# Pooled attention and a gated product on one core: the first w3 tile in two halves, and 71 steps in other places of the written order

## The chip, the core and the metric

The kernel runs on one core of a Trainium2 chip. The metric is the device time in microseconds (us). TensorE (PE) does the matmuls and transposes, VectorE (DVE), ScalarE (ACT) and GpSimd (POOL) the elementwise work, and SyncE (SP) issues the transfers between memory and the core.

## What is computed

The reference, cut to its core (the weights come as float64):

```
k_p = k.reshape(8, 8, 72, 8, 64).mean(axis=3)      # 576 tokens pooled to 72 keys
v_p = v.reshape(8, 8, 72, 8, 64).mean(axis=3)
attn = softmax(q @ k_p^T / 8)                      # 8 batches, 8 heads
x = (attn @ v_p), heads side by side               # 4608 x 512
a = x @ w1;  b = x @ w2                            # w1, w2: 512 x 1024
out = ((a * b) @ w3) @ w_out                       # w3: 1024 x 1024, w_out: 1024 x 512
```

## The kernel before

**W phase.** The kernel first forms W = w3 @ w_out, so that each token needs only (a*b) @ W. A float64 tile is loaded as pairs of 32-bit words. ACT converts the high word (`high`, line L190), ACT or DVE takes the bits of the low word (`low`, L196 on ACT, L199 on DVE), and DVE joins them (`conv_b`, L203). w3 comes in 16 tiles (s = 0 to 15). PE turns each one by four transposes (`w_turn`, L253 or L255), ACT rounds the turned tile into its high part (`w3_hi`, L265), and the low part is the rest: for tiles in `LO3_PE` PE subtracts (`w3_sub`, one matmul at L258) and ACT copies (`w3_lo`, L273), for the others DVE subtracts (L261). The tiles of w_out take `ro_high`, `ro_low`, `ro_conv`, `ro_hi` (L239) and `ro_lo` (L243). Twelve matmuls per tile (`w_mm`, L1068) add three passes (high by high, high by low, low by high) for each of four column blocks. Transposes of the identity whose result nobody reads (`warm`, L281) occupy PE before the first product.

**Chunks.** The 4608 tokens are 12 chunks of 384. Chunks 0 to 3 are done plainly (`a_mm`, `b_mm` at L787, `b_post` at L807, `g_lo` at L817, `out_mm` at L835). The others go in pairs M = 2 to 5 with seven products per column block j (`prod(M, j, i)`, L976) in the manner of Strassen. Mixed weights for these (`mix_sum` L881, `mix` L887 to L889) are formed once on POOL or DVE and stored in `ws`. For each pair `load_u(M, j, g)` (L958) brings group g of block j into a ring: groups 0, 1 and 2 are 512 KB each and share five slots, group 3 is 256 KB with a slot of its own. Group 1 serves the products i = 2 and 4, group 0 those with i = 0 and 1. `out_some(m, j, ...)` (L851) adds to the output of a chunk, `out_post` stores it.

**Attention.** For chunk n `tr_q` (L390) turns q, `s_mm` (L543) makes scores, `soft1` to `soft4` the softmax, `prep_k`, `prep_v`, `prep_v3` (L499), `vr_sub` and `prep_vr2` (L530) prepare the pooled keys and values for the products at L739. `load_k`, `load_v` and `load_vr` bring them in.

**What sets the order.** The program is a list `plan` of steps. A tuple of numbers says in which order they are issued, and every engine works through its own instructions in that order. All loads and most stores pass through SP's queue. Eight completion semaphores go round among the transfers, so a transfer is issued only when the one eight places ahead has landed, and when its buffer is free.

```
    for i in SEQUENCE:
        fn, args = plan[i]
        fn(*args)
```

Of the kernel before, what the change touches and what calls it, by code (L numbers as in the profile page):

```python
# [8 lines left out]
F32 = mybir.dt.float32  # L9
# [10 lines left out]
def kernel(  # L20
# [46 lines left out]
    LO3_PE = [0, 2, 3, 4, 6, 7]  # L67
# [12 lines left out]
        "r3_low": {(0,), (1,), (2,), (4,), (13,), (15,)},  # L80
# [91 lines left out]
    def load_w3(s):  # L172
        h, j = divmod(s, NJ)
        raw["w3", s] = raw_cell(s % 4)
        nc.sync.dma_start(
            out=raw["w3", s].rearrange("p (i c) -> p i c", i=4),
            in_=w3r[h * 512:(h + 1) * 512, 2 * j * P:2 * (j + 1) * P].rearrange("(i p) c -> p i c", p=P))
# [27 lines left out]

    def w_tiles(s):
        if s == NJ + 4:
            t = early.tile([P, 24], F32, name="space")
            nc.gpsimd.memset(t, 0.0)
        if "wt" not in stage:  # L210
            stage["wt"] = [t[:, i] for t, x in (
                (p1.tile([P, x, 512], I32, tag=tag, name="wt"), x)
                for tag, x in (("PTh", 3), ("PTx", 4))) for i in range(x)]
        if s < NJ:
            stage["wo", s] = stage["wt"][s % 4], f(stage["wt"][4 + s % 3])
        stage["w3", s] = W_cell(0, 4 + s % 4, I32), W_cell(1, 4 + s % 4, F32)

    def r3_high(s):
        w_tiles(s)
        high(raw["w3", s], stage["w3", s][1])  # L220

    def r3_low(s):
        low(raw.pop(("w3", s)), stage["w3", s][0], other("r3_low", s))

    def r3_conv(s):
        conv_b(*stage["w3", s])
# [20 lines left out]
    def w_turn(s):  # L247
        r = f(stage.pop(("w3", s))[0])
        ps = tp[s] = patt.tile([P, 512], F32, tag="att", name="att")
        for it in range(4):  # L250
            o, i = ps[:, it * P:(it + 1) * P], r[:, it * P:(it + 1) * P]
            if s in LO3_PE:
                nc.tensor.matmul(out=o, lhsT=i, rhs=ident, is_transpose=True, start=it == 0, stop=it == 3)  # L253
            else:
                nc.tensor.transpose(out=o, in_=i, identity=ident)  # L255
# [7 lines left out]
    def w3_hi(s):  # L263
        w3t[s] = hl_cell(4 + s % 4)
        nc.scalar.copy(out=w3t[s][0], in_=tp[s])  # L265

    def w3_sub(s):
        if s in LO3_PE:
            less(tp[s], w3t[s][0])

    def w3_lo(s):
        if s in LO3_PE:
            nc.scalar.copy(out=w3t[s][1], in_=tp.pop(s))  # L273
        else:
            minus(w3t[s][1], tp.pop(s), w3t[s][0])
# [884 lines left out]
    for i in range(1, 7):  # L1160
        at("L", F0 - 5, warm, i, 5)
    for u in range(NJ + 2):
        k = F0 + 2 * (u - 2)
        if u < NJ:
            at("P", k, r3_high, u)
            at("P", k, r3_low, u)
            at("P", k, ro_high, u)
# [4 lines left out]
        if u < NJ:  # L1172
            at("P", k, r3_conv, u)
        if 1 <= u < NJ + 1:
            at("P", k, w_turn, u - 1)
            at("P", k, w3_hi, u - 1)
# [4 lines left out]
        if 1 <= u < NJ + 1:  # L1181
            at("P", k, w3_sub, u - 1)
            at("P", k, ro_hi, u - 1)
            at("P", k, w3_lo, u - 1)
    for s in range(NS):
        k = F0 + 2 * s
        if s < NJ:
            at("L", k - 11, load_w3, s)
# [144 lines left out]
    for b in range(1, B):  # L1333
# [189 lines left out]
```

## Time and profile before

| | us |
|---|---|
| median of 3 runs | 742.46 (741.91 to 743.19) |
| the profiled execution | 740.11 |
| its span | 738.3 |
| PE busy in the span | 720.7 |
| DVE, ACT, POOL busy | 523.8, 362.1, 189.1 |

The span is what the trace shows from the first to the last instruction; 1.8 us of the profiled execution lie outside it. PE is busy nearly all the time, so a gap of PE is what an order can remove.

### The profile page before, as it was taken

To read this page: it belongs to the slowest core of one execution; us is meant where nothing else is said; L and a number is where in the kernel's file an instruction comes from. 1 tells how busy PE (TensorE), PEld (TensorE's weight loads), DVE (VectorE), ACT (ScalarE), POOL (GpSimd) and SP (SyncE) were. 2 spreads that over 40 slices of the span, in tenths; PEclk is the share of its full clock that TensorE was granted. 3 is DMA by queue.
4 is the path that set the end of the run, shared out by engine and by line. 5 is a ranking of instruction groups with operands and counts; after the bars stand their busy time and mean duration, and the time that the engine had idled before them with its cause. 6 is when DMAs were issued, how large, how long until landed. Compare 5 with 4: busy or idle time off the path is not lost.

```text
span 738.3 us, 12016 instructions
## 1 busy us (share of the span) xinstructions
PE 720.7 (98%) x3992; PEld 665.9 (90%) x3992; DVE 523.8 (71%) x1042; ACT 362.1 (49%) x1140; POOL 189.1 (26%) x241
## 2 busy tenths in 40 slices
PE   7999999999999999998999999999999999999997
PEld 6788989899989999998999899899898999899996
DVE  3988898869767968887568877488887576643342
ACT  6888786534334544663355553355554254421221
POOL 2343865434506506203313011220030100000000
PEclk9999999999999999999999999999999999999999
DMA  9999590174457556798785739966358563166511
GB/s 320 348 285 288 154 255 30 59 205 118 108 141 249 155 152 194 198 293 224 221 263 151 186 106 277 252 204 175 86 194 276 139 208 115 34 228 233 173 35 69
DMA packets 138733, 136.59 MB, mean 185 GB/s; under 512 B 76080, under 2 KB 104240, under 8 KB 138672
## 3 DMA queue, kind: packets, MB, share of 16 engines
q1 hardware_dynamic: 138528, 135.69, 63.0%
q8 instruction: 32, 0.52, 0.3%
q14 instruction: 29, 0.24, 0.1%
q10 hardware_dynamic: 144, 0.13, 0.1%
HBM read 99.35 MB, written 24.12 MB: 167 GB/s over the span
## 4 chain that ended last, share of the span: by engine, by line
PE 78%; DVE 9%; DMA 4%; POOL 4%; ACT 3%; issue 2%; SPq 0%; DVEq 0%; POOLq 0%; ACTq 0%
PE a L976 17%; PE o L835 14%; PE att L976 8%; PE o L851 8%; PE a L787 6%; PE b L787 6%; PE b L976 5%; PE att L543 4%; PE att L739 4%; PE o L1068 3%; DMA ring<-ws 2%; DMA PTx<-T 1%; DVE mx L559 1%; POOL VR L530 1%; DMA raw<-in_moe_w_out_dram 1%
## 5 line engine op out<-in xcount | busy, mean ns | idle before, releaser
L976 PE MATMUL a<-X,ring 128*128 128x384 f32 x768 | 157.0, 340 | 1.4 <-DVE g L1009 0.7
L976 PEld LDWEIGHTS a<-X,ring 128*128 128x128 f32 x768 | 134.7, 189 | 7.0 <-DVE g L1009 1.7
L835 PE MATMUL o<-Wc,gh 128*128 128x512 f32 (+1 forms) x384 | 118.6, 390 | 0.0
L581 ACT ACTIVATE E<-att,mx 128x72 f32<-128x72 f32 (+1 forms) x264 | 80.7, 324 | 32.8 <-DVE mx L559 21.2
L482 POOL TENSOR_TENSOR st<-st 72x512 f32<-72x512 f32 (+2 forms) x32 | 42.7, 1335 | 162.0 <-DMA st<-in_v_dram 101.3
L835 PEld LDWEIGHTS o<-Wc,gh 128*128 128x128 f32 x384 | 70.2, 188 | 11.7 <-DVE ob L868 0.2
L976 PE MATMUL att<-X,ring 128*128 128x384 f32 x384 | 78.6, 341 | 2.0 <-DMA ring<-ws 2.0
L835 PE MATMUL o<-Wc,gl 128*128 128x512 f32 (+1 forms) x192 | 74.6, 389 | 1.2 <-DVE gl L817 1.1
L787 PE MATMUL b<-xT,hl 128*128 128x384 f32 x384 | 73.2, 340 | 0.1
L787 PE MATMUL a<-xT,hl 128*128 128x384 f32 x384 | 72.4, 337 | 0.0
L976 PEld LDWEIGHTS att<-X,ring 128*128 128x128 f32 x384 | 68.0, 190 | 3.5 <-DVE R L630 2.4
L787 PEld LDWEIGHTS a<-xT,hl 128*128 128x128 f32 x384 | 66.7, 188 | 0.5
L787 PEld LDWEIGHTS b<-xT,hl 128*128 128x128 f32 x384 | 66.2, 188 | 0.7 <-DVE a L807 0.4
L851 PE MATMUL o<-Wc,gh 128*128 128x512 f32 x192 | 61.6, 393 | 0.0
L817 DVE TENSOR_TENSOR gl<-a,gh 128x384 fp32r<-128x384 f32 x64 | 41.1, 646 | 22.7 <-ACT gh L812 18.2
L581 ACT ACTIVATION_READ_ACCUMULATOR E<-att,mx 128x1 f32 (+1 forms) x264 | 55.2, 209 | 0.0
L812 ACT CAST gh<-a 128x384 fp32r<-128x384 f32 x64 | 33.0, 517 | 43.8 <-DVE a L1004 14.9
L543 PE MATMUL att<-kbd,qT 128*128 128x144 f32 (+1 forms) x320 | 49.3, 286 | 0.6 <-DVE qT L390 0.6
L543 PEld LDWEIGHTS att<-kbd,qT 128*128 128x128 f32 (+1 forms) x320 | 45.3, 179 | 2.9 <-DVE qT L390 0.9
L835 PEld LDWEIGHTS o<-Wc,gl 128*128 128x128 f32 x192 | 36.0, 188 | 10.2 <-DVE gl L817 2.6
L559 DVE TENSOR_REDUCE mx<-att 128x4 f32<-128x288 f32 (+1 forms) x80 | 34.9, 448 | 14.4 <-PE att L543 14.3
L982 ACT COPY a<-a 128x384 f32<-128x384 f32 x32 | 15.3, 479 | 51.5 <-PE a L976 51.3
(164 smaller groups left out, 1348.7 us busy)
## 6 DMA issues: line engine op xcount, KB each, us to landing
ring<-ws SPq DMA_DIRECT2D x81, 512.0 KB
raw<-in_moe_w_dram SPq DMA_DIRECT2D x32, 512.0 KB
ws<-hl SPq DMA_DIRECT2D x24, 512.0 KB
out_dram<-ob SPq DMA_DIRECT2D x35, 256.0 KB
st<-in_v_dram SPq DMA_DIRECT2D x16, 512.0 KB
PTx<-T SPq DMA_DIRECT2D x28, 288.0 KB
ring<-ws SPq DMA_DIRECT2D x29, 256.0 KB
st<-in_k_dram SPq DMA_DIRECT2D x24, 288.0 KB
```

The costliest lines, as they stand in the source:

```text
L482: eng.tensor_tensor(out=t[:, :, 0:4], in0=t[:, :, 0:4], in1=t[:, :, 4:8], op=ALU.add)
L543: nc.tensor.matmul(out=ps[:nt, 2 * KP * j:2 * KP * (j + 1)], lhsT=qT[n][:, pr, off:off + nt], rhs=kbd[b % 2][:, pr], start=True, stop=True,)
L559: nc.vector.tensor_reduce(out=mx[:nt, hs], in_=sv, axis=AX.X, op=ALU.min)
L581: nc.scalar.activation(out=E[:nt, h], in_=sv[:, i], func=AF.Exp, scale=-1.0, bias=mx[:nt, h:h + 1], accum_out=sm[:nt, h:h + 1])
L739: nc.tensor.matmul(out=Tp[n, pr, "x"][:, off:off + cnt], lhsT=parts[x][0], rhs=parts[x][1], start=x == 0, stop=x == 3)
L787: nc.tensor.matmul(out=o, lhsT=w12[j, w][:, kt, sw], rhs=x[sx][:, kt], start=(i == 0), stop=(i == 3 * NK - 1))
L812: nc.scalar.copy(out=gh, in_=g)
L817: eng.tensor_tensor(out=gl, in0=g, in1=f(gh), op=ALU.subtract)
L835: nc.tensor.matmul(out=o, lhsT=(gh, gl)[sg][:, c], rhs=W[j][sw][:, d], start=(j == 0 and i == 0), stop=(j == NJ - 1 and i == 2))
L851: nc.tensor.matmul(out=oacc[m][t], lhsT=(gh, gl)[sg][:, t * P:(t + 1) * P], rhs=W[j][sw], start=(j == first and i == 0), stop=(j == last a ...
L976: nc.tensor.matmul(out=o, lhsT=w[:, kt, sw], rhs=x[sx][:, kt], start=first and n == 0, stop=n == 5, skip_group_check=True)
L1068: nc.tensor.matmul(out=wacc[h][it], lhsT=w3t[s][sa][:, it * P:(it + 1) * P], rhs=wo[j][sb], start=(j == 0 and i == 0), stop=(j == NJ - 1 a ...
```

## The change

The tile s = 0 of w3 is handled in halves of 256 columns (`HALVED`): two transfers of 256 KB, two conversions, twice two transposes, two roundings. It leaves `LO3_PE`, so DVE subtracts its low part in halves, and its matmul at L258 and copy at L273 are gone. Its low word moves from ACT to DVE. The tiles `wt` for w_out are taken ahead of the first use. Lines after the start shift by 9 to 13.

```
-    LO3_PE = [0, 2, 3, 4, 6, 7]
+    LO3_PE = [2, 3, 4, 6, 7]
+    HALVED = (0,)
-        "r3_low": {(0,), (1,), (2,), (4,), (13,), (15,)},
+        "r3_low": {(1,), (2,), (4,), (13,), (15,)},
...
+    def load_w3(s, *y):
         h, j = divmod(s, NJ)
+        if not any(y):
+            raw["w3", s] = raw_cell(s % 4)
+        i = slice(2 * y[0], 2 * y[0] + 2) if y else slice(0, 4)
...
+        minus(w3t[s][1][:, cols(y)], tp[s][:, cols(y)], w3t[s][0][:, cols(y)])
...
+    def in_parts(*x):
+        for y in [(0,), (1,)] if x[-1] in HALVED else [()]:
+            at(*x, *y)
...
     SEQUENCE = (
-        103, 104, 7, 9, 107, 108, 0, 1, 8, 115, 10, 11, 12, 18, 3, 111, 2, 4, 5, 19, 119, 123, 13, 14, 21, 22,
+        1656, 0, 110, 27, 40, 111, 7, 8, 112, 9, 115, 116, 123, 10, 119, 127, 1, 11, 14, 12, 21, 13, 22, 3, 15,
```

Of the order, the three places below matter most. First DVE's start, where L203 joins the words of a tile, L243 and L261 subtract. Before:

```order
1 L121 TENSOR_REDUCE msk<-ident 128x4
2 L203 SCALAR_TENSOR_TENSOR Wc<-Wc 128x512
3 L203 SCALAR_TENSOR_TENSOR wt<-wt 128x512
4 L243 TENSOR_TENSOR hl<-wt,hl 128x512
5 L203 SCALAR_TENSOR_TENSOR Wc<-Wc 128x512
6 L203 SCALAR_TENSOR_TENSOR wt<-wt 128x512
7 L199 TENSOR_SCALAR Wc<-raw 128x512
```

And now (L208 is the former L199, L212 the former L203, L272 the former L261, L253 the former L243):

```order
1 L122 TENSOR_REDUCE msk<-ident 128x4
2 L208 TENSOR_SCALAR Wc<-raw 128x256 x2
3 L212 SCALAR_TENSOR_TENSOR Wc<-Wc 128x256 x2
4 L212 SCALAR_TENSOR_TENSOR wt<-wt 128x512
5 L272 TENSOR_TENSOR hl<-att,hl 128x256
6 L253 TENSOR_TENSOR hl<-wt,hl 128x512
7 L212 SCALAR_TENSOR_TENSOR Wc<-Wc 128x512
8 L272 TENSOR_TENSOR hl<-att,hl 128x256
```

DVE takes the low word itself, in halves, joins both halves ahead of everything else, and subtracts the first tile's low part around `ro_lo(0)`. On PE the 20 and 5 unread transposes that stood around `w3_sub(0)` stand together.

Second, POOL at batch 1 (R is softmax work, vbd `prep_v3`, VR `prep_vr2`, the tile st at L482 `prep_k`). Before:

```order
51 L514 TENSOR_TENSOR st<-st 32x2x128
52 L630 TENSOR_TENSOR R<-E,R 96x64 x2
53 L499 TENSOR_TENSOR vbd_1_106<-vm,vbd_0_105 64x4x64
54 L881 TENSOR_TENSOR mix<-hl 128x256 x2
55 L530 TENSOR_SCALAR VR_108<-vrh,msk 128x2x64 x4
56 L887 TENSOR_TENSOR mix<-mix 128x2x128
57 L888 TENSOR_TENSOR mix<-mix 128x128
58 L889 TENSOR_TENSOR mix<-mix 128x128
59 L482 TENSOR_TENSOR st<-st 72x2x256
60 L483 TENSOR_TENSOR st<-st 72x2x128
61 L484 TENSOR_TENSOR km<-st 72x128
62 L499 TENSOR_TENSOR vbd_1_106<-vm,vbd_0_105 64x4x64
```

And now:

```order
51 L526 TENSOR_TENSOR st<-st 32x2x128
52 L893 TENSOR_TENSOR mix<-hl 128x256 x2
53 L642 TENSOR_TENSOR R<-E,R 96x64 x2
54 L511 TENSOR_TENSOR vbd_1_106<-vm,vbd_0_105 64x4x64
55 L899 TENSOR_TENSOR mix<-mix 128x2x128
56 L900 TENSOR_TENSOR mix<-mix 128x128
57 L901 TENSOR_TENSOR mix<-mix 128x128
58 L511 TENSOR_TENSOR vbd_1_106<-vm,vbd_0_105 64x4x64
59 L542 TENSOR_SCALAR VR_108<-vrh,msk 128x2x64 x4
60 L494 TENSOR_TENSOR st<-st 72x2x256
```

The second `prep_v3` no longer stands behind the four VR instructions and `prep_k`, and the two sums of `mix_sum(0,0)` stand ahead of the softmax.

Third, SP in the pair M = 2 (L958 loads a ring tile, 128x512 is the group of 256 KB). Before:

```order
125 L958 DMA ring<-ws 128x1024
126 L407 DMA st<-in_k_dram 72x2x512
127 L958 DMA ring<-ws 128x1024
128 L407 DMA st<-in_k_dram 72x2x512
129 L958 DMA ring<-ws 128x512
130 L958 DMA ring<-ws 128x1024
131 L477 DMA st<-in_v_dram 16x1x512 x4
132 L869 DMA out_dram<-ob 128x512
133 L958 DMA ring<-ws 128x1024 x2
```

And now:

```order
124 L970 DMA ring<-ws 128x1024
125 L419 DMA st<-in_k_dram 72x2x512 x2
126 L970 DMA ring<-ws 128x512
127 L970 DMA ring<-ws 128x1024
128 L489 DMA st<-in_v_dram 16x1x512 x4
129 L970 DMA ring<-ws 128x1024 x3
130 L419 DMA st<-in_k_dram 72x2x512
131 L881 DMA out_dram<-ob 128x512
```

`load_u(2,3,1)` stood in row 127 and is now the first of row 129, behind `load_u(2,1,3)` (row 126), `load_u(2,2,1)` (row 127) and `load_vr(4)`, and ahead of `load_u(2,2,0)` and `load_u(2,2,2)`. The store `out_post(3,2)` moved behind them. On PE the products of that place, from `out_some(4,0,2,8)` on, were `prod` (2,2,2), (2,1,6), (2,2,4), (2,2,1), (2,2,0) and are now (2,1,6), (2,2,2), (2,2,0), (2,2,1), (2,2,4).

Other moves that the prediction speaks of, all by the numbers of the order: on DVE `r3_conv(5)` stands ahead of `ro_conv(3)`, `g_lo(0,0)` and `b_post(0,1)` ahead of `prep_k(1,2)`, `tr_q(3,2)` ahead of `mix(2,0)` and `soft1(3,0,0)`, and `b_post(2,1)` ahead of `mix_lo(3,0)`; `prep_v2(2,0)` on ACT stands much earlier.

## Rows read from the trace of the kernel before

**Rows 1.** The page: busy time of each engine, its share, instructions.

```profile
PE 720.7 (98%) x3992; PEld 665.9 (90%) x3992; DVE 523.8 (71%) x1042; ACT 362.1 (49%) x1140; POOL 189.1 (26%) x241
```

**Rows 2.** Waits of PE, whole span: line, releaser, us in total, times, longest.

```profile
PE att L976 <- DMA ring<-ws: 2.0, 1, 2.0
...
PE att L739 <- POOL vbd L499: 1.2, 1, 1.2
PE att L255 <- DVE Wc L203: 1.1, 1, 1.1
PE o L835 <- DVE gl L817: 1.1, 2, 0.8
PE att L258 <- ACT hl L265: 1.1, 1, 1.1
PE att L739 <- ACT vbd L494: 0.8, 1, 0.8
...
PE att L543 <- DVE qT L390: 0.6, 1, 0.6
PE a L976 <- ACT tmp L990: 0.3, 1, 0.3
```

**Rows 3.** Timeline of PE at the start: start, us, operation, count, idle before.

```profile
1.34 5.59 PE L281 MATMUL b<-ident 128*128 128x128 f32 x25 [1.34 <-POOL ident masks.py:199]
8.26 0.66 PE L253 MATMUL att<-ident,Wc 128*128 128x128 f32 x4 [1.33 <-DVE Wc L203]
8.76 2.35 PE L281 MATMUL b<-ident 128*128 128x128 f32 x20
...
11.64 2.44 PE L1068 MATMUL o<-hl 128*128 128x512 f32 x9
```

**Rows 4.** Timeline of ACT at the start.

```profile
4.18 0.68 ACT L190 ACTIVATE Wc<-raw 128x512 f32<-128x512 f32 x1 [1.86 <-DMA raw<-in_moe_w_dram]
6.28 0.66 ACT L190 ACTIVATE wt<-raw 128x512 f32<-128x512 f32 x1 [1.42 <-DMA raw<-in_moe_w_out_dram]
```

**Rows 5.** Timeline of DVE, 0 to 30 us.

```profile
7.52 0.69 DVE L203 SCALAR_TENSOR_TENSOR Wc<-Wc 128x512 int32<-128x512 int32 x1 [5.91 <-ACT Wc L196]
...
21.86 0.69 DVE L203 SCALAR_TENSOR_TENSOR Wc<-Wc 128x512 int32<-128x512 int32 x1
```

**Rows 6.** Busy time by stretch: length, PE, PEld, DVE, ACT, POOL, granted clock, DMA share, GB/s.

```profile
0.00:30.00 30.00, 25.03 (x133) 20.92 (x134) 16.56 (x28) 24.40 (x44) 5.75 (x15) 1.00 0.98 338
...
340.00:345.00 5.00, 3.33 (x10) 3.36 (x11) 2.08 (x5) 1.14 (x3) 0.00 (x0) 0.66 0.87 284
```

**Rows 7.** Timeline of POOL around batch 1.

```profile
118.49 0.69 POOL L630 TENSOR_TENSOR R<-E,R 96x64 fp32r<-96x64 f32 x2 [9.62 <-ACT R L625]
...
120.08 3.21 POOL L881 TENSOR_TENSOR mix<-hl 128x256 f32<-128x256 f32 x2
123.28 3.08 POOL L530 TENSOR_SCALAR VR<-vrh,msk 128x128 fp32r<-128x128 f32 x4
```

**Rows 8.** Timeline of DVE, 105 to 135 us.

```profile
106.50 1.79 DVE L203 SCALAR_TENSOR_TENSOR wb<-wb 128x512 int32<-128x512 int32 x1
...
111.72 0.68 DVE L203 SCALAR_TENSOR_TENSOR wb<-wb 128x512 int32<-128x512 int32 x1
```

**Rows 9.** The chain that ended last, 328 to 347 us: start, us, what.

```profile
332.65 1.05 PE a L976 x6
...
333.72 7.82 DMA ring<-ws
...
341.67 2.26 PE att L976 x6
343.93 1.60 PE a L976 x6
```

**Rows 10.** Timeline of SP's queue at the ring load.

```profile
331.15 2.89 SPq L958 DMA_DIRECT2D ring<-ws  x2
...
339.67 1.03 SPq L958 DMA_DIRECT2D ring<-ws  x2
```

More of the change, by code (lines that the diff above doesn't have):

```diff
@@ L170, in load_wo, with cols, raw_cols @@
         nc.sync.dma_start(out=raw["wo", j], in_=wor[j * P:(j + 1) * P, :])
-    def load_w3(s):
+    def cols(y):
+        return slice(256 * y[0], 256 * y[0] + 256) if y else slice(0, 512)
+    def load_w3(s, *y):
         h, j = divmod(s, NJ)
-        raw["w3", s] = raw_cell(s % 4)
+        if not any(y):
+            raw["w3", s] = raw_cell(s % 4)
+        i = slice(2 * y[0], 2 * y[0] + 2) if y else slice(0, 4)
         nc.sync.dma_start(
-            out=raw["w3", s].rearrange("p (i c) -> p i c", i=4),
-            in_=w3r[h * 512:(h + 1) * 512, 2 * j * P:2 * (j + 1) * P].rearrange("(i p) c -> p i c", p=P))
+            out=raw["w3", s].rearrange("p (i c) -> p i c", i=4)[:, i],
+            in_=w3r[h * 512:(h + 1) * 512, 2 * j * P:2 * (j + 1) * P].rearrange("(i p) c -> p i c", p=P)[:, i])
+    def raw_cols(s, y):
+        return raw["w3", s].rearrange("p (c t) -> p c t", t=2)[:, cols(y)].rearrange("p c t -> p (c t)")
     def load_w12(j, w):
@@ L204, in conv_b @@
             out=r, in0=z.bitcast(I32), scalar=3, in1=r, op0=ALU.logical_shift_left, op1=ALU.bitwise_or)
+    wt = [t[:, i] for t, x in (
+        (p1.tile([P, x, 512], I32, tag=tag, name="wt"), x)
+        for tag, x in (("PTh", 3), ("PTx", 4))) for i in range(x)]
+    for i in range(NJ):
+        stage["wo", i] = wt[i % 4], f(wt[4 + i % 3])
     def w_tiles(s):
@@ L209, in w_tiles, with r3_high, r3_low, r3_conv @@
             nc.gpsimd.memset(t, 0.0)
[L210 to L215, printed above, removed]
-        stage["w3", s] = W_cell(0, 4 + s % 4, I32), W_cell(1, 4 + s % 4, F32)
[L218 to L226, printed above, removed]
+        stage["w3", s] = W_cell(0, 4 + s % 4, I32), W_cell(1, 4 + s % 4, F32)
+    def r3_high(s, *y):
+        if not any(y):
+            w_tiles(s)
+        high(raw_cols(s, y), stage["w3", s][1][:, cols(y)])
+    def r3_low(s, *y):
+        low(raw_cols(s, y), stage["w3", s][0][:, cols(y)], other("r3_low", s, *y))
+    def r3_conv(s, *y):
+        conv_b(*(x[:, cols(y)] for x in stage["w3", s]))
     def ro_high(s):
@@ L245, with w_turn @@
     tp = {}
[L247 to L251, printed above, removed]
+    def w_turn(s, *y):
+        r = f(stage["w3", s][0])
+        if not any(y):
+            tp[s] = patt.tile([P, 512], F32, tag="att", name="att")
+        for it in range(2 * y[0], 2 * y[0] + 2) if y else range(4):
+            o, i = tp[s][:, it * P:(it + 1) * P], r[:, it * P:(it + 1) * P]
             if s in LO3_PE:
@@ L261, in minus, with w3_hi, w3_sub, w3_lo @@
         nc.vector.tensor_tensor(out=out, in0=ps, in1=f(part), op=ALU.subtract)
[L263 to L267, printed above, removed]
+    def w3_hi(s, *y):
+        if not any(y):
+            w3t[s] = hl_cell(4 + s % 4)
+        nc.scalar.copy(out=w3t[s][0][:, cols(y)], in_=tp[s][:, cols(y)])
+    def w3_sub(s, *y):
         if s in LO3_PE:
             less(tp[s], w3t[s][0])
-    def w3_lo(s):
+    def w3_lo(s, *y):
         if s in LO3_PE:
-            nc.scalar.copy(out=w3t[s][1], in_=tp.pop(s))
+            nc.scalar.copy(out=w3t[s][1], in_=tp[s])
         else:
-            minus(w3t[s][1], tp.pop(s), w3t[s][0])
+            minus(w3t[s][1][:, cols(y)], tp[s][:, cols(y)], w3t[s][0][:, cols(y)])
     def warm(i, n):
@@ L1164 @@
         if u < NJ:
-            at("P", k, r3_high, u)
-            at("P", k, r3_low, u)
+            in_parts("P", k, r3_high, u)
+            in_parts("P", k, r3_low, u)
             at("P", k, ro_high, u)
@@ L1172 @@
         if u < NJ:
-            at("P", k, r3_conv, u)
+            in_parts("P", k, r3_conv, u)
         if 1 <= u < NJ + 1:
-            at("P", k, w_turn, u - 1)
-            at("P", k, w3_hi, u - 1)
+            in_parts("P", k, w_turn, u - 1)
+            in_parts("P", k, w3_hi, u - 1)
         if u == 0:
@@ L1181 @@
         if 1 <= u < NJ + 1:
-            at("P", k, w3_sub, u - 1)
+            in_parts("P", k, w3_sub, u - 1)
             at("P", k, ro_hi, u - 1)
-            at("P", k, w3_lo, u - 1)
+            in_parts("P", k, w3_lo, u - 1)
     for s in range(NS):
@@ L1187 @@
         if s < NJ:
-            at("L", k - 11, load_w3, s)
+            in_parts("L", k - 11, load_w3, s)
             at("L", k - 11, load_wo, s)
```

291 rows, old and new, of the table SEQUENCE are left out of this document.

## The prediction

> **What bounds the kernel now.** The page comes first: PE is busy 720.7 us of the span of 738.3 [rows 1]. No other engine is above 71%, so the time can fall only where PE stands idle or runs at the lower clock, 17.6 us of gaps in all. No matmul of weight goes away, so the next view is the list of what PE waits for [rows 2]. It is a short list of single waits, none longer than 2.0 us, each at its own place: one for a joined word on DVE and one for a rounded tile on ACT (the W phase; the first turn's own wait stands in [rows 3]), two for `g_lo`, two for the pooled values (vbd), one for a turned q, one for a ring load. The reader should see that nearly every one of them is alone on its line, so each is worth what the order does at that one place.
>
> The third view is the timeline of PE at the start [rows 3]. Its 25 unread transposes end at 6.93 (1.34 + 5.59), then it waits 1.33 for the joined first tile, and the first product starts at 11.64. ACT began on w3 at 4.18, when the load landed, and on w_out at 6.28, also on landing; DVE's join came at 7.52 [rows 4, 5]. The last view is the ring load of pair M = 2: SP issues it at 333.72, it lands 7.82 us later, PE starts at 341.67 [rows 9], and in the window from 340 to 345 the granted clock is 0.66 on average [rows 6]. In the first 30 us, with waits of up to 1.33, it is 1.00. Of its two levels the chip here fell to the lower, 1.2 GHz, behind the longest wait, so this wait costs more than its 2.0: the twelve matmuls after it took 2.26 + 1.60 us against 1.05 for six at full clock [rows 9], 1.76 us. That is 3.75 us at one place.
>
> **The change, part by part.**
>
> *The first tile.* The load of 512 KB landed at about 4.16. The DMA engines moved 338 GB/s in this stretch [rows 6], so 256 KB is 0.78 us and the first half is there near 3.4, the second near 4.2 (half a us later if one more issue of SP shows; two take 1.03 [rows 10]). DVE takes the low word itself in halves, ACT the high one in halves (about half of 0.68 each [rows 4]), and DVE's two half joins (about half of 0.69 each [rows 5]) are done between 5 and 6 instead of at 8.2. So the turn no longer waits: PE goes from 6.93 into four transposes (0.50 from start to start) and 25 unread ones. Twenty of them took 2.35 [rows 3], so 25 take 2.7 to 2.9, and the first product can start at 10.1 to 10.4 against 11.64; the matmul at L258 that stood between is gone. Its inputs are ready by then: ACT has w_out at 6.28 and needs two operations of 0.66, DVE's join of 0.69 follows (8.3, as before), rounding and rest are about 0.6 each, 9.5. Here the gain is 1.2 to 1.5.
>
> Whether the later tiles keep it is the next question. In the second and third tile PE waited 1.1 for L265 and 1.1 for the join of 21.86 [rows 2, 5]. ACT has no `w3_lo(0)` and no low word of tile 0 any more (two operations like the 0.66 less ahead of these), and `r3_conv(5)` stands ahead of `ro_conv(3)`, so the second of these waits should shrink. But the DMA engines are at 98% of this stretch [rows 6], the loads come no earlier, and PE arrives earlier: some of the gain is waited away. Bounds: 0.8 (half of the 1.5 waited away) and 2.0 (all of it, and half of the second wait). I take 1.6, near the top, since both named waits are for engines that have less to do.
>
> What speaks against the split is a rule of the Trainium skill, "DMA: Bandwidth & Descriptors", section Bandwidth, that transfers should be batched to 1 MiB or more for three quarters of the peak. By it the two halves would come later than the whole did, this term would lie at its lower bound and the whole sum below at 4.9. The trace has 338 GB/s with transfers of 512 KB there and none of 256 KB, so no row bears the rule out for this split.
>
> *Chunk 0's `g_lo` and `b_post`.* The two waits of L835 for L817 are 1.1 together [rows 2]. DVE now does `g_lo(0,0)` and `b_post(0,1)` ahead of `prep_k(1,2)`, five instructions that fold keys. What is late next is these keys; they serve chunk 2's scores, far behind. Bounds 0 and 1.1, I take 0.8.
>
> *POOL at batch 1.* PE waited 1.2 for vbd [rows 2]. That instruction stood behind four VR instructions (3.08) and `prep_k`; now both stand behind it, and the two sums (3.21) fill an idle time of 9.62 [rows 7]. The wait should go: 1.0, bounds 0 and 1.2. What is late next is VR, by less than the 0.7 of vbd.
>
> The sums now run beside DVE between 109 and 118. DVE's join took 1.79 at 106.50, with POOL in a subtraction, and 0.68 at 111.72, with POOL idle [rows 8]: work on POOL slows DVE. By these rows the two sums can cost DVE 1.1 us each, and `g_lo` hangs on DVE there; this is in the allowance below. The Trainium skill, "GPSIMD Engine Reference", section Key points, says that the two share their SBUF interfaces, with contention where DVE reads two SBUF inputs, and so speaks against this move; the trace agrees with its 1.79 against 0.68.
>
> *Turned q and vbd in chunk 3.* These waits are 0.6 and 0.8 [rows 2]. `tr_q(3,2)` comes earlier, but `mix(2,0)` now stands ahead of the softmax step that frees PE's bank, so of the 0.6 I count half. For vbd of L494, ACT does `prep_v2(2,0)` far earlier: all 0.8. Sum 1.1, bounds 0.3 and 1.4.
>
> *The ring load of M = 2.* Ring tiles of 512 KB share five slots. `load_u(2,3,1)` held a slot and 512 KB of queue ahead of `load_u(2,2,1)`, which got its slot only when the products of 332.65 to 333.70 had freed one, and was the second of SP's two issues that begin at 331.15 [rows 10]. Now it takes the slot that `load_u(2,3,1)` took before, and is issued right behind `load_u(2,1,3)`, at about 331.5: two us earlier, and behind 512 KB less. It lands by 339.5. PE also does `prod(2,1,6)` first (1.05), so it needs it only at 340.7. This wait goes, with its clock. What is late next is `load_u(2,2,0)`: `prod(2,2,0)` is now third instead of fifth, due at about 341.8. Before it was issued at 339.67, behind the store, and waited for a lane [rows 10]; now the lane is free earlier and the store is behind it, but `load_u(2,3,1)` stands ahead of it. Its slot (the products of block 1) is free at about 337, so it is issued between 337 and 339. At the 284 GB/s of that stretch [rows 6] 512 KB take 1.8; with 3 us in all it lands at 340 to 342; with the 7.82 of the other [rows 9] at 345. So the gain lies between 3.75 (no wait) and minus 1.1 (a wait of 3.1, and the clock lost again, 1.76). I take 2.7, nearer to the first, since its queue is emptier.
>
> *All other moves.* About fifty, most of them one place up or down beside idle time. A step that goes up makes another late. The shortest waits on the list are 0.3 [rows 2]; I allow five such and nothing for gains: minus 1.5, bounds 0 and minus 4 (with the contention above, 2.2).
>
> **Sum.** 1.6 + 0.8 + 1.0 + 1.1 + 2.7 - 1.5 = 5.7 us. The profiled span of 738.3 becomes 732.6 and the profiled execution of 740.11 about 734.4. That execution lies 2.35 below the median of 742.46, whose runs reach from 741.91 to 743.19, so I carry the difference over: 736.8.
>
> **The rivals.**
>
> 1. *The ring wait only moves.* `load_u(2,2,0)` lands at 345, PE waits 3.1 us at `prod(2,2,0)` and the clock falls again. For it: the DMA share of 0.87 there and the 7.82 [rows 6, 9]. Against it: the issue is earlier and the store is out of the way. The term becomes -1.1, the gain 1.9: 740.6. Still faster.
>
> 2. *The start is given back.* PE arrives earlier at each tile, but tiles arrive as before; everything gained by 12 us is waited away by 25, since the loads are at 98% of the engines [rows 6]. Against it: the waits named in that stretch are for ACT and DVE, not for a load [rows 2]. The gain is 4.1 instead of 5.7: 738.4.
>
> 3. *New waits eat the rest.* Steps are moved on all engines, and PE's order too. If nineteen of the moves give a wait of 0.3, that is 5.7 instead of 1.5 and the gain falls to 1.5; with twenty-four (7.2) it is nothing: 742.5; from twenty-nine on it is slower. For it: PE is busy 98% of the span [rows 1], so whatever an engine delivers later shows soon. Against it: all gaps of PE together are 17.6 now, with far more steps than those moved.
>
> 4. *Slower.* One load of the ring decides: `load_u(2,2,0)`, with `prod(2,2,0)` as the place. Apart from the ring the sum is 3.0, and the wait removed gives 3.75; a new wait w costs w + 1.76. The time is 1.5 above the old one when w passes 6.5, that is when the load lands after 348.3, 11 us after its issue at 337. That needs its slot to be freed late too, since `load_u(2,3,1)` may hold the issue on SP until the slot for itself is free: then the loads of a block wait for products behind them. At w = 8 it gives 745.5.
>
> **How the numbers follow.** The forecast as summed, between 734 and 739.5 in its own range (terms at their bounds by twos): 0.58. Rival 1: 0.13, faster. Rival 2: 0.06, faster. Rival 3 ends within 1.5 us in 0.13 and slower in 0.04. Rival 4: 0.06. A difference of 0.2%, 1.5 us here, is about what a measurement of this kernel can tell from none. So faster is 0.77, same 0.13, slower 0.10. The best bounds together would be 2.0 + 1.1 + 1.2 + 1.4 + 3.75 = 9.5, or 733.0. The range from 733.6 to 742.0 leaves that corner, the slower cases and part of the third out.
>
> **What would show it.** Right: no wait of PE between 6.93 and the first turn, first product near 10.2, the products near 30 us earlier by 1 to 2; the waits for L817, vbd on POOL and vbd on ACT gone from the list; no ring wait near 340, and a granted clock of 1.00 in 340 to 345. Wrong: a wait for a ring load at `prod(2,2,0)` of more than 2 us with a lower clock behind it; more than six new waits on the list; waits of PE's sources on loads in the first 40 us. The order alone cannot tell what DVE and POOL do to each other in 108 to 132, and that is where I am least sure after the ring.

## The result, and the profile after

The changed kernel takes 731.22 us in the median of 4 runs (730.1 to 732.16), the kernel before 742.18 (738.33 to 743.19). The ratio is 0.9861, with a 95% interval from 0.9822 to 0.99, so the change saves about 10 us. The forecast was 736.8, in a range from 733.6 to 742.0. The way was right and the size was not: the gain is nearly twice the 5.7 us forecast. The profiled execution took 732.16, its span is 730.2.

The page and PE's waits over the whole span, in the views of [rows 1] and [rows 2]. L988 is the former L976, L847 the former L835, L1080 the former L1068.

```profile
PE 717.1 (98%) x3991; PEld 664.6 (91%) x3991; DVE 525.8 (72%) x1047; ACT 361.0 (49%) x1140; POOL 192.8 (26%) x241
```

```profile
PE b L988 <- DMA ring<-ws: 2.4, 1, 2.4
PE b L293 <- POOL ident masks.py:199: 1.3, 1, 1.3
PE att L269 <- ACT hl L277: 1.3, 2, 0.7
PE o L847 <- DVE gl L829: 0.9, 2, 0.6
PE att L266 <- ACT hl L285: 0.7, 1, 0.7
PE a L988 <- DVE g L1021: 0.6, 1, 0.6
PE a L988 <- ACT tmp L1002: 0.3, 1, 0.3
PE att L264 <- DVE Wc L212: 0.3, 1, 0.3
PE o L1080 <- ACT hl L249: 0.3, 1, 0.3
...
```

The reader should see three things. PE's wait for the first turn is gone, and so are both waits for vbd and the one for a turned q. The longest wait is still a ring load, 2.4 us instead of 2.0, and it is now in the product (2,2,0), which writes the bank b.

The waits for `g_lo` add up to 0.9 where they were 1.1, but they are not the same two. The one that the move of `g_lo(0,0)` aimed at is gone, the one of 0.35 near 109 stays (0.32 at 107.77), and one is new. Before, then after:

```profile
92.97 0.50 PE L835 MATMUL o<-Wc,gl 128*128 128x512 f32 x1 [0.77 <-DVE gl L817]
```

```profile
121.13 0.50 PE L847 MATMUL o<-Wc,gl 128*128 128x512 f32 x1 [0.55 <-DVE gl L829]
```

The new one stands where POOL now works beside DVE, first in the two sums that were moved up, then in the mixes that follow them (L899 to L901, 118.74 to 121.40). Before, POOL was idle until 118.49 [rows 7]. DVE before, then POOL and DVE after:

```profile
116.50 0.43 DVE L199 TENSOR_SCALAR wb<-raw 128x512 int32<-128x512 int32 x1
...
120.85 0.55 DVE L817 TENSOR_TENSOR gl<-a,gh 128x384 fp32r<-128x384 f32 x1
```

```profile
114.48 2.55 POOL L893 TENSOR_TENSOR mix<-hl 128x256 f32<-128x256 f32 x2 [7.18 <-DVE sm L613]
```

```profile
116.35 0.95 DVE L208 TENSOR_SCALAR wb<-raw 128x512 int32<-128x512 int32 x1
...
120.27 0.81 DVE L829 TENSOR_TENSOR gl<-a,gh 128x384 fp32r<-128x384 f32 x1
```

These two of DVE's operations take 0.95 and 0.81 where they took 0.43 and 0.55. PE reaches this place 1.6 us earlier than before (119.86 instead of 121.43), but `g_lo` is done only 0.3 earlier (121.08 instead of 121.40).

PE's timeline at the start, as in [rows 3], and ACT's and DVE's rows that answer to [rows 4, 5]:

```profile
1.34 5.59 PE L293 MATMUL b<-ident 128*128 128x128 f32 x25 [1.34 <-POOL ident masks.py:199]
6.73 0.64 PE L266 MATMUL att<-ident,Wc 128*128 128x128 f32 x4
7.21 2.89 PE L293 MATMUL b<-ident 128*128 128x128 f32 x25
10.38 0.50 PE L1080 MATMUL o<-hl 128*128 128x512 f32 x1 [0.28 <-ACT hl L249]
...
25.74 0.50 PE L269 MATMUL att<-hl,neg 128*128 128x512 f32 x1 [0.66 <-ACT hl L277]
```

```profile
7.71 0.67 ACT L199 ACTIVATE wt<-raw 128x512 f32<-128x512 f32 x1 [3.11 <-DMA raw<-in_moe_w_out_dram]
...
24.55 0.66 ACT L199 ACTIVATE Wc<-raw 128x512 f32<-128x512 f32 x1 [1.35 <-DMA raw<-in_moe_w_dram]
```

```profile
3.41 1.54 DVE L208 TENSOR_SCALAR Wc<-raw 128x256 int32<-128x256 int32 x2 [1.80 <-DMA raw<-in_moe_w_dram]
4.87 0.74 DVE L212 SCALAR_TENSOR_TENSOR Wc<-Wc 128x256 int32<-128x256 int32 x2
```

The first half landed at 3.4 and both halves were joined at 5.6, as worked out; the first product starts at 10.38 instead of 11.64. But the first w_out tile came at 7.71 instead of 6.28, so PE waits 0.28 for its rounding ahead of that product, and at 24.55 ACT waits for a load.

Both traces hold every matmul of PE, in the order of the program, so the end of one step can be read in both by counting. The difference grows like this in the two profiled executions:

| step of PE | end before | end after | difference |
|---|---|---|---|
| last turn of w3 | 65.40 | 65.40 | 0.0 |
| first `out_mm` | 94.86 | 93.69 | 1.2 |
| first product with values, chunk 1 | 132.24 | 129.61 | 2.6 |
| the same, chunk 3 | 209.61 | 204.96 | 4.7 |
| the same, chunk 5 | 304.49 | 299.98 | 4.5 |
| first `out_some` behind the ring load | 348.88 | 343.33 | 5.6 |
| `prod(3,3,0)` | 473.20 | 466.74 | 6.5 |
| `prod(4,2,6)` | 565.46 | 557.38 | 8.1 |

In this pair the start gives nothing by 65 us, the steps from there to chunk 3 give 4.7 (1.2, 1.5 and 2.0) where the forecast had 2.9, the ring gives 1.0, and 2.5 come later, where the forecast had only losses. One pair of executions is not enough for these shares, as the experiments show: the start by itself is worth more than nothing, and the chunks by themselves less than 4.7.

### The profile page after: what moved, and what is told of

It reads as the page before. It is cut to its first block, busy times and chain, and to the rows that moved or that the text cites. A ratio compares the mean times of both kernels' runs of the same rounds, so it can differ in the third digit from the quotient of the medians.

```text
span 730.2 us, 12027 instructions
## 1 busy us (share of the span) xinstructions
PE 717.1 (98%) x3991; PEld 664.6 (91%) x3991; DVE 525.8 (72%) x1047; ACT 361.0 (49%) x1140; POOL 192.8 (26%) x241
## 4 chain that ended last, share of the span: by engine, by line
PE 79%; DVE 8%; DMA 5%; ACT 3%; issue 2%; POOL 1%; SPq 0%; DVEq 0%; ACTq 0%; POOLq 0%
PE a L988 17%; PE o L847 15%; PE o L863 9%; PE att L988 9%; PE a L799 7%; PE b L799 6%; PE att L751 5%; PE b L988 4%; PE att L555 4%; PE o L1080 2%; DMA raw<-in_moe_w_dram 1%; DVE wb L212 1%; DMA st<-in_k_dram 1%; DMA ring<-ws 1%; DMA raw<-in_moe_w_out_dram 1%
## 5 line engine op out<-in xcount | busy, mean ns | idle before, releaser
L988 PE MATMUL a<-X,ring 128*128 128x384 f32 x768 | 156.1, 339 | 0.9 <-DVE g L1021 0.6
L988 PEld LDWEIGHTS a<-X,ring 128*128 128x128 f32 x768 | 134.3, 188 | 5.6 <-DVE g L1021 0.9
L847 PE MATMUL o<-Wc,gh 128*128 128x512 f32 (+1 forms) x384 | 118.5, 390 | 0.0
L847 PEld LDWEIGHTS o<-Wc,gh 128*128 128x128 f32 x384 | 70.2, 188 | 11.6 <-DVE ob L880 0.2
L988 PE MATMUL att<-X,ring 128*128 128x384 f32 x384 | 77.3, 338 | 0.0
L847 PE MATMUL o<-Wc,gl 128*128 128x512 f32 (+1 forms) x192 | 74.5, 388 | 0.9 <-DVE gl L829 0.9
L988 PEld LDWEIGHTS att<-X,ring 128*128 128x128 f32 x384 | 67.4, 188 | 1.0
L847 PEld LDWEIGHTS o<-Wc,gl 128*128 128x128 f32 x192 | 36.0, 188 | 9.8 <-DVE gl L829 2.4
L571 DVE TENSOR_REDUCE mx<-att 128x4 f32<-128x288 f32 (+1 forms) x80 | 34.8, 447 | 10.6 <-PE att L555 10.6
```

The source lines that it names most:

```text
L571: nc.vector.tensor_reduce(out=mx[:nt, hs], in_=sv, axis=AX.X, op=ALU.min)
L847: nc.tensor.matmul(out=o, lhsT=(gh, gl)[sg][:, c], rhs=W[j][sw][:, d], start=(j == 0 and i == 0), stop=(j == NJ - 1 and i == 2))
L988: nc.tensor.matmul(out=o, lhsT=w[:, kt, sw], rhs=x[sx][:, kt], start=first and n == 0, stop=n == 5, skip_group_check=True)
```

## The experiments

Each kernel was timed in five rounds beside the kernel before; the times of before in these rounds have medians of 740.4 to 741.2. Seven of the twelve are made in one way: the order of before is cut into stretches, and some of them take the changed order. Every such edit has this form:

```
-    SEQUENCE = (the order of before)
+    SEQUENCE = (the steps of one stretch in the changed order, all others in the order of before)
```

**Where the gain lies: four stretches, each by itself.** First the start (steps 0 to 291 of 2679, with the code of the halves).

> The kernel before with the change's code and its order only for the steps up to about 66 us (the halved first tile and the W phase); every later step in the order of before. Theory 1 (the gain is a sum of single waits at their own places, and the start is given back by 26 us because the loads come later): product 1 starts about 1.3 us earlier, the gain is under 0.3 us at 60 us, and the time is that of before within 0.5 us. Rival (the start's gain of 1.6 carries to the end): 1.2 to 2 us faster.

Measured: 738.57, ratio 0.9964 (0.9942 to 0.9986), that is 1.0 to 4.3 us faster. Theory 1 falls, though the two profiled executions had suggested it.

Then the middle (steps 292 to 1202).

> The kernel before with only the steps between about 66 and 318 us in the order of the change (g_lo and b_post, vbd, the turned q). Theory 1: about 4.5 us faster, with the waits for L817, vbd on POOL, vbd on ACT and the turned q gone. Rival (the loss of the clock drop at the ring load is most of the gain, the rest is scatter between executions): under 2 us faster.

Measured: 738.37, ratio 0.9962 (0.9941 to 0.9982), 1.3 to 4.4 us faster. PE's waits of that kernel between 60 and 330 us:

```profile
PE att L739 <- DVE PTx L707: 1.0, 2, 0.8
PE o L835 <- DVE gl L817: 0.9, 2, 0.6
```

The waits for vbd (1.2 and 0.8) and for the turned q (0.6) of [rows 2] are gone. New are a wait for PTx and, within the 0.9, the one of 0.55 for `g_lo` near 121. The interval leaves out the 4.5 us of theory 1 by a little, but not a gain under 2 us, so this run alone does not refute the rival that the clock at the ring is most of the gain; the run with the whole ring below does.

The loads of pair M = 2 (steps 1203 to 1310), and all that is later.

> The kernel before with only the steps around the ring loads of block 2 in pair M = 2 (about 318 to 357 us) in the order of the change. Theory 1: about 1 us faster in the trace, with a wait of 2 to 2.5 us at the product (2,2,0) in place of the one at (2,2,2). Rival (clock drop): 3.5 us or more faster, granted clock 1.00 in 340 to 345. If the new wait drops the clock again: 0.7 us slower.

Measured: 739.9, ratio 0.9988 (0.9967 to 1.0008), between 2.4 us faster and 0.6 slower, so the rival's 3.5 falls. This kernel has the new order of the loads and the old order of the products.

> The kernel before with only the steps after about 357 us in the order of the change. Theory 1: about 2.5 us faster, with the waits near 472 (ring load, 0.75), 494 (g, 0.73) and 561 to 564 (0.6) gone or smaller; none of these was in the prediction's sum. Prediction's own view (such moves cost 1.5 us): slower by 0 to 1.5 us.

Measured: 741.48, ratio 1.0005 (0.998 to 1.003). The cut fell between the loads of block 2, which are in the third stretch, and its products on PE, which are in the fourth. So this kernel has the changed order of products and the old order of loads, and pays for it, as its list of waits shows:

```profile
PE b L976 <- DMA ring<-ws: 4.1, 1, 4.1
```

`prod(2,2,0)` comes third, and its load still stands behind the store. The two have to be moved together, and the stretches were cut anew.

**The ring as a whole, and the rest.** The first has the order of loads on SP and of products on PE (steps 1203 to 1464), the second only what comes behind.

```
 SP:  load_u(2,1,3), load_u(2,2,1), load_vr(4)
-SP:  load_u(2,3,1), ahead of these
+SP:  load_u(2,3,1)
 SP:  load_u(2,2,0), load_u(2,2,2)
-PE:  prod (2,2,2), (2,1,6), (2,2,4), (2,2,1), (2,2,0)
+PE:  prod (2,1,6), (2,2,2), (2,2,0), (2,2,1), (2,2,4)
```

> The kernel before with both parts of the change at pair M = 2, the order of the loads on SP and the order of the products on PE (the two earlier runs split them: loads alone, products with all that is late). Theory 2 (the two need each other): 2 to 3.5 us faster than before, with one ring wait of 0 to 2.5 us at product (2,2,0) and no lower clock. Rival (they add as measured apart, -0.9 and +0.4): 0 to 1 us faster.

Measured: 740.53, ratio 0.9997 (0.9973 to 1.002). The wait is 2.4 us at (2,2,0); the ring is worth nothing that can be measured.

> The kernel before with only the steps from the middle of pair M = 2 on (after about 385 us) in the order of the change, without the ring loads and products of block 2. Theory 2 (these moves give what the prediction's sum lacks): 1.5 to 3 us faster, with the waits for the ring load near 472 and for g near 494 gone or halved. Prediction's view: slower by 0 to 1.5 us.

Measured: 738.42, ratio 0.9972 (0.9948 to 0.9995), 0.4 to 3.9 us faster. PE's waits from 400 us on in that kernel, and what stood there before:

```profile
PE a L976 <- ACT tmp L990: 0.3, 1, 0.3
```

```profile
PE b L976 <- DMA ring<-ws: 0.7, 1, 0.7
PE a L976 <- DVE g L1009: 0.7, 1, 0.7
PE a L976 <- ACT tmp L990: 0.3, 1, 0.3
PE a L976 <- DVE tmp L1001: 0.3, 1, 0.3
```

The moves among the late products take away a ring wait, a wait for g and a wait for tmp, and add none. This does not rest on one pair: behind 400 us the waits of PE over 0.1 us add up to 1.1 to 2.4 in the six traces with the old order there, and to 0.3 to 1.0 in the eight with the new one.

**The change again, and without parts of it.**

> The changed kernel once more, beside the next three on the same chip. Expected 730 to 732, 8 to 11 us under the kernel before in the same rounds.

Measured: 731.07, ratio 0.9875 (0.9848 to 0.9902).

> The changed kernel without its start: steps up to about 66 us and the first tile as before, all later ones as changed. Theory 2 (the start alone was worth 1 to 4 us in the run of the start by itself, and adds to the rest): 1.5 to 2.5 us slower than the changed kernel, 733 median. Theory 1 (the start is given back by 26 us): same as the changed kernel within 0.5 us.

Measured: 734.66, ratio 0.9921 (0.9894 to 0.9949): leaving the start out costs 3.6 us between the medians. With the 2.7 by itself, the start is worth about 3 us, twice the forecast.

**Why the ring wait stays.**

```
-SP:  load_u(2,3,1), load_u(2,2,0), load_u(2,2,2)
+SP:  load_u(2,2,0), load_u(2,3,1), load_u(2,2,2)
```

> The changed kernel with one more step moved: the load (2,3,1) behind the load (2,2,0) instead of ahead of it. Theory (the 2.45 us wait of product (2,2,0) comes from the 512 KB and the slot ahead of its load): the wait falls to under 0.5 us and the kernel is 1.5 to 2.5 us faster than the changed one. Rival (the load of keys whose landing frees the lane decides): the wait stays over 1.5 us and the time is the same.

Measured: 730.52, ratio 0.986 (0.9831 to 0.9889), no different from the changed kernel; the wait is still 1.7, and the changed kernel's second trace has 1.8 there. The chain at that place, first of the changed kernel, then of this one:

```profile
323.97 8.87 DMA st<-in_k_dram
...
332.91 6.76 DMA ring<-ws
...
339.71 1.31 PE b L988 x6
```

```profile
321.46 7.25 DMA st<-in_k_dram
...
328.77 8.06 DMA ring<-ws
...
336.88 1.31 PE b L988 x6
```

Both theories were half right. In both of these traces a load of keys holds the lane, until 332.85 or 328.71. (In the second trace of the changed kernel the issue comes at 331.92, right behind products of PE, and the load takes 6.73.) Measured against PE, which is 2.1 us further here (`prod(2,1,6)` ends at 334.17 instead of 336.22), the ring load is issued 2.1 us earlier. But it then takes 8.06 us instead of 6.76. The window of the changed kernel (length, PE busy, granted clock, DMA share, GB/s) has the engines of the queue at 96%; an earlier place bought little there:

```profile
335.00:345.00 10.00, 7.55 (x42) 1.00 0.96 292
```

**What the start is worth, and by what.** The first kernel takes the split of the transfer away and leaves the rest of the halves.

```
-        i = slice(2 * y[0], 2 * y[0] + 2) if y else slice(0, 4)
+        if any(y):
+            return
+        i = slice(0, 4)
```

> The changed kernel with the first w3 tile loaded in one transfer of 512 KB again, still converted, turned and rounded in halves. Theory (what counts at the start is DVE taking the low word and PE not waiting, not the split transfer): same as the changed kernel within 0.5 us, the first turn still without a wait, 731. Rival (the half that lands early is what removes the wait): the first turn waits again and the time is 1 us or more above the changed kernel.

Measured: 732.49, ratio 0.9886 (0.9858 to 0.9913), against 0.9875 with the split. Its start:

```profile
1.34 4.67 PE L295 MATMUL b<-ident 128*128 128x128 f32 x25 [1.34 <-POOL ident masks.py:199]
5.85 0.60 PE L268 MATMUL att<-ident,Wc 128*128 128x128 f32 x4
6.28 2.89 PE L295 MATMUL b<-ident 128*128 128x128 f32 x25
8.93 2.77 PE L1082 MATMUL o<-hl 128*128 128x512 f32 x9
```

The first turn has no wait either, so the split transfer is not needed for it. What is left is the conversion in halves, and that DVE takes the low word at once, where ACT took it behind w_out (DVE's join of 7.52 waited for L196 [rows 5]). No run tells these two apart.

The second kernel is the kernel before with unread transposes in place of the wait.

```
-    at("L", F0 - 5, warm, 0, 20)
+    at("L", F0 - 5, warm, 0, 34)
```

> The kernel before with 14 more unread transposes ahead of the first turn and nothing else (39 instead of 25, about 1.5 us more), which fill the wait of 1.3 to 2.7 us that PE has there. Theory 3 (the start is worth more than its 1.6 us because in some executions the granted clock falls behind this wait): the first product comes no earlier than in the best executions of before, but the time is 0.5 to 2 us lower in the median, and no execution has a lowered clock between 9 and 13 us. Rival (only the earlier tile counts): same as before, or 0.5 us slower.

Measured: 739.45, ratio 0.9981 (0.9964 to 0.9999), 0.1 to 2.7 us faster although the first turn, at 8.36, comes no earlier than the 8.26 of [rows 3]. Of its start one row shows the cover, with 39 transposes, and the next the first turn:

```profile
1.34 6.46 PE L281 MATMUL b<-ident 128*128 128x128 f32 x39 [1.34 <-POOL ident masks.py:199]
8.36 0.66 PE L253 MATMUL att<-ident,Wc 128*128 128x128 f32 x4 [0.55 <-DVE Wc L203]
8.85 2.35 PE L281 MATMUL b<-ident 128*128 128x128 f32 x20
```

Against it stands the start of the experiment with the whole ring, which has the start of before:

```profile
8.49 0.66 PE L253 MATMUL att<-ident,Wc 128*128 128x128 f32 x4 [2.02 <-DVE Wc L203]
8.99 4.01 PE L281 MATMUL b<-ident 128*128 128x128 f32 x20
...
13.54 0.71 PE L1068 MATMUL o<-hl 128*128 128x512 f32 x2
```

and its windows (length, PE busy, granted clock, DMA share, GB/s):

```profile
0.00:9.00 9.00, 5.64 (x30) 1.00 0.79 270
9.00:13.00 4.00, 4.00 (x23) 0.57 1.08 352
```

The turn waited 2.02 instead of 1.33, the granted clock fell to 0.57, the 20 transposes took 4.01 instead of 2.35, and the first product came at 13.54 instead of 11.64. The profiled execution of before was one without this. The wait is longer here although the turn comes only 0.2 later: the 25 unread transposes ended at 6.48 instead of 6.93.

**Both small repairs together.** One transfer for the first tile, and the load (2,3,1) behind (2,2,0).

> The changed kernel with the first w3 tile loaded in one transfer again and the load (2,3,1) behind (2,2,0). Theory (each was the same as the changed kernel within its interval; w_out then lands earlier and the ring wait is shorter): 729 to 731, ratio 0.983 to 0.988 against before. Rival (PE arrives earlier at the ring, which is full, and waits the gain away): 731 to 732.5, no better than the changed kernel.

Measured: 730.73, ratio 0.9876 (0.9849 to 0.9903). It is no better than the changed kernel.

## Why the prediction was wrong

| term | forecast | measured by itself |
|---|---|---|
| first tile and W phase | 1.6 | 2.7 (1.0 to 4.3); 3.6 when left out |
| chunks 0 to 3 (three terms) | 2.9 | 2.8 (1.3 to 4.4) |
| ring load of M = 2 | 2.7 | 0.2 (-1.5 to 2.0) |
| all other moves | -1.5 | 2.1 (0.4 to 3.9) |
| sum | 5.7 | 7.8; the whole 9.3 (7.3 to 11.3) |

The measured gains are the ratios times 741 us. Their sum lies within the interval of the whole. The ring and the late moves have intervals as wide as their terms, so the order of the misses below goes by the medians.

- **"All other moves: minus 1.5" is the term that failed most.** It counted five new waits of 0.3 and "nothing for gains". Of the former, the list of the changed kernel has a few of 0.2 to 0.3, mostly in the W phase, and the one of 0.55 for `g_lo`; of the latter there were some 2 us. The waits for the ring near 472 and for g near 494 were in the trace of before, 0.7 each, and the prediction does not name them. At 494 the change takes `out_some(6,3,0,1)` and `out_some(6,3,1,2)` from behind the products there to ahead of the one that waited, `prod(3,1,1)`. Near 472 neither PE's order nor SP's is changed within 20 us, so how that wait went is not shown. Rival 3, which went further in this direction, falls with it.
- **"I carry the difference over" failed beside the terms.** In the profiled executions the span was forecast at 732.6 and measured at 730.2, a miss of 2.4. The prediction then added 2.35, by which the profiled execution of before lay under the median of three. The changed kernel's lies 0.94 above its median. So some 3.3 of the 5.6 us between 736.8 and 731.22 come from this step. Against the 740.8 that is the median of 84 executions of before, the profiled one lay only 0.7 low.
- **The first tile was mis-sized.** That the first turn stops waiting was right. That the first product starts at 10.1 to 10.4 came out (10.38), but in part by luck: its inputs were to be ready by 9.5, and PE waited for them until 10.38. That 1.6 of it stays was read from one execution, in which the unread transposes ended at 6.93 and the wait of 1.33 left the clock alone. In the seven traces with the start of before they end between 5.66 and 6.93, while the turn waits for the joined tile until 8.3 to 8.8 in all of them. So the wait is 1.33 to 2.72; behind 2.02 and 2.45 the clock fell, behind the other five it did not. Their first product starts at 11.6 to 13.5. In the six traces with the changed start PE goes on when the transposes end, and the first product starts at 8.9 to 10.6. The last turn of w3 then ends at 62.8 to 65.4, with the start of before at 65.4 to 67.8. So rival 2 (the start is given back), which looked right in the two profiled executions with 0.0 at 65 us, is refuted by the timing and by the other traces.
- **The split transfer was not needed.** It came with a late w_out tile in two of its four traces (7.71 and 7.89) and not in the other two (6.39 and 6.43). The Trainium skill, "DMA: Bandwidth & Descriptors", section Bandwidth, has the rule that speaks against it, to batch transfers to 1 MiB or more. The run with one transfer shows no difference in the whole, so going against the rule cost nothing here that was measured.
- **The ring: the step "with 3 us in all it lands at 340 to 342" failed.** The load was issued at 332.91, which with PE 4.5 us ahead is the 337 assumed, and landed 6.76 us later. The 7.82 of [rows 9] was nearer to the right price (6.7 to 7.9 in the five traces with this order of loads and products), and it was set aside because the queue was thought emptier. The wait at (2,2,2) went, as predicted, and one of 2.4 at (2,2,0) took its place: rival 1 in its mechanism, though its further price was wrong. It added 1.76 for the clock to every new wait; here a wait of 2.45 cost no clock, though one of 2.37 without the start did. Of the 1.76, 0.26 is not the clock: behind that wait six matmuls took 1.31 at full clock, not 1.05. The 3.75 to be won was too high as well: of the five traces with the old order there, only the one of before lost the clock at this place.
- **Chunks 0 to 3 came out as a sum, not in each part.** Vbd and q gave all of theirs. `g_lo` gave the 0.77 that was aimed at, and lost 0.55 again near 121, beside POOL's sums and mixes: DVE needed 0.95 and 0.81 for two operations that took 0.43 and 0.55 before. That is the contention that the allowance held. The wait stands in all seven traces with the changed middle (0.55 to 0.57) and in none of the others; no run moves POOL's sums and mixes alone, so that they are its cause is read from the rows and not tested.
- **Rival 4 (slower)** needs a wait of over 6.5 us. The order of products without the order of loads had one of 4.1; that kernel lost about what its late moves gain by themselves (2.1) and came out the same as before.

What stays open is how the remaining 1.5 us between the sum and the whole are to be divided. It is within the intervals, and no run was made for it.

## What to carry to other kernels

When PE is at 98%, list all its waits and go through the order at each, the ones under 1 us too: here three of 0.3 to 0.7 were worth more than the largest one, by the medians. A wait in a place where transfers are full was not removed by a better place in the queue; the load took longer from there. And a single profiled execution shows one draw: of a clock that may or may not fall after a wait, and of how long the wait is. Look at the same place in several traces before a wait gets its price, and do not carry one execution's distance from the median over to another kernel.

## What the runs showed of the hardware

- **The length of a wait did not decide whether the clock fell.** At the ring load near 340 us, in different kernels and executions, the granted clock fell to half at waits of 1.99, 2.37 and 4.08 us, fell a microsecond after the end of one of 2.39, and stayed at 1.00 behind 2.13, 2.30, 2.45 and 3.04. The row pair below is of the change without its start (wait of 2.37, clock lost) and then of the changed kernel (2.45, clock kept):

```profile
341.65 2.29 PE L976 MATMUL b<-X,ring 128*128 128x384 f32 x6 [2.37 <-DMA ring<-ws]
```

```profile
339.71 1.31 PE L988 MATMUL b<-X,ring 128*128 128x384 f32 x6 [2.45 <-DMA ring<-ws]
```

- **The clock goes with about half of the scatter of the kernel before.** Over the 84 executions of before beside the experiments, the mean granted clock and the time have a correlation of -0.73, and the time rises by 0.67 us for each 0.001 of clock lost. The 31 executions with a clock of 0.999 or more have a median of 739.34, the 20 with 0.996 or less one of 742.69. With the wait at the start filled, none of 12 was at 0.996 or less, where that share would give about three.
- **Work on POOL can slow DVE.** In the trace of before the `g_lo` operation of DVE runs 96 times. In the 76 cases with POOL idle it takes 0.52 to 0.56. In the 20 cases beside POOL it takes 0.51 to 1.65, and over 0.6 in 11 of them. Not every operation of POOL does it: the 0.55 at 120.85 above ran beside a sum, which POOL began at 120.08 [rows 7].
